# Attention decode on one core: K of a query in one load instead of two, and the output projection of all heads moved behind the last V

## The chip, the core and the metric

The kernel runs on one core of a Trainium2 chip. A core has a matrix engine (PE; loading its stationary operand is shown as PEld), a vector engine (DVE), a scalar engine (ACT), a general engine (POOL) and a sync engine (SP), which here does nothing but issue transfers. Transfers run on 16 DMA engines that all queues share. SBUF is the on-chip memory of 128 partitions, PSUM the 128-partition memory that PE writes. The metric is device microseconds (us) of one execution. 1 KB is 1024 bytes in the sizes of loads below; MB and GB/s are decimal.

## The reference, cut to what matters

One token for each of two batch rows goes through a pre-norm attention over a long cache and a bilinear gated feed-forward. All data are float32.

```python
B, D, H, Sk, Dh, F = 2, 448, 16, 8192, 256, 1792
q = (layernorm(x) @ wq).reshape(B, 1, H, Dh)            # one query a head and batch row
scores = einsum("bhqd,bhkd->bhqk", q, k_cache) * Dh**-0.5
o = einsum("bhqk,bhkd->bhqd", softmax(scores), v_cache)
h = x + o.reshape(B, 1, H * Dh) @ wo
n = layernorm(h)
out = h + ((n @ w_gate) * (n @ w_up)) @ w_down
```

K and V are 16 heads x 2 batch rows x 8192 x 256 float32 each, 268 MB each. Everything else is 24 MB.

## The kernel before, in words

The program is one stream of 32 queries (`NQ`), a query being one head `h` and one batch row `b`. SP issues every large load in program order, and a load waits in SP's queue until the buffer that it overwrites is free; all that is queued behind it on SP waits too.

**Buffers.** `ring` holds four buffers of 32 KB a partition. A query takes all four in turn: two halves of K (`load_k`, 4096 KB each) and two halves of V (`load_v`, 4096 KB each; the last V goes in four loads of 2048 KB). Query weights and output weights of two heads come together, 1792 KB every fourth query (`load_w`, two buffers of their own in `wpool`).

**One query.** PE computes the scores from a K half as it lands (`scores`, L185: 16 matmuls of 512 columns a half, four of them side by side on 32 columns of the array each; a float32 matmul shows as two records, so a half is "x32" in the profile). The 8192 scores lie as 128 partitions x 2048 in one PSUM tile `s` of four banks. DVE takes the maximum of each half (L241), PE transposes the two results (L245), DVE reduces and negates (L247), PE spreads it to all partitions (L251), ACT copies it (L253) and computes the exponentials `p` with their row sums (L255). Then DVE multiplies V with `p` and sums, eight instructions of 128x2048 a query (L263). Around every second query PE also computes the next head's query vectors (`queries`, L165 and L168).

**Output projection.** When both queries of a head are done, `output` finishes it between the two score halves of the next query: row sums (L195), reciprocal (L197), the sum over partition groups (L200), the division (L204), and ten matmuls that add the head's share into `acc_ps` (L210, stationary operand 128x128 weights, moving operand 2 columns). The last head's `output` stands behind the loop.

**Feed-forward.** `load_ff` puts the gate, up and down weights (3136 KB each) into `ring` buffers behind the last V. Then `hT` (L291), the second layer norm (`center`, `squares`, L295 to L300), gate projection (L312 on `wg_t`), its scale `rv` (L320 to L326), the residual into the result's PSUM (L333), up projection (L312 on `wu_t`), their product (L342), transposes (L344, L346), down projection (L351: 56 matmuls of 112 columns, the result on four column groups), copy (L358) and two output transfers (L361).

Of the kernel before, what the change touches and what calls it, by code (L numbers as in the profile page):

```python
# [14 lines left out]
EPS = 1e-5  # L15
P = 128
# [6 lines left out]
HK = GK // 2  # L23
NO = DH // R
MM = 512
RING = 4
WQ, WO = 3 * DH + P, 2 * D
WH = WQ + WO
# [5 lines left out]
OC = D // G  # L34
# [10 lines left out]
def tile_decode_block(  # L45
# [5 lines left out]
    wqo: bass.AP,  # L51
# [8 lines left out]

    nc = tc.nc
    const = ctx.enter_context(tc.tile_pool(name="const", bufs=1))
    ring = ctx.enter_context(tc.tile_pool(name="ring", bufs=RING))
    wpool = ctx.enter_context(tc.tile_pool(name="wpool", bufs=2))
# [6 lines left out]
    def load_w(hp):  # L71
        t = wpool.tile([P, 2, WH], F32, tag="w", name=f"w_{hp}")
        nc.sync.dma_start(t.rearrange("p h n -> p (h n)"), wqo[hp])
        return t

    def load_k(b, h):
        got = []
        for n in range(2):
            t = ring.tile([P, 2, G, HK], F32, tag="ring", name=f"k_{h}_{b}_{n}")
            nc.sync.dma_start(t.rearrange("p c g k -> p (c g k)"), kc[b, h, n])  # L80
            got.append(t)
        return got

    def load_v(b, h, parts):
        got = []
        for n in range(2):
            t = ring.tile([P, NO // 2, GK], F32, tag="ring", name=f"v_{h}_{b}_{n}")
            k = NO // 2 // parts
            for m in range(parts):
                nc.sync.dma_start(  # L90
                    t[:, m * k : (m + 1) * k, :].rearrange("p o k -> p (o k)"),
                    vc[b, h, n, :, m * k * GK : (m + 1) * k * GK],
                )
            got.append(t)
        return got
# [3 lines left out]
    w_now = load_w(0)  # L99
# [3 lines left out]
    avg = const.tile([P, P], F32, name="avg")  # L103
    nc.vector.memset(avg, 1.0 / D)
    ones = const.tile([P, P], F32, name="ones")
    nc.vector.memset(ones, 1.0 / R)
    row = const.tile([1, P], F32, name="row")
    nc.vector.memset(row, 1.0)
# [5 lines left out]

    acc_ps = ps_1.tile([P, DC, B], F32, name="acc_ps")
# [12 lines left out]
    def center(h, tag):  # L128
        mean = ps_m.tile([P, B], F32, tag="sm", name=f"mean_{tag}")
        nc.tensor.matmul(mean, avg, over_chunks(h, f"h_{tag}"), start=True, stop=True)  # L130
        xc = const.tile([P, DC, B], F32, name=f"xc_{tag}")
        nc.vector.tensor_sub(xc, h, mean[:, None, :].to_broadcast([P, DC, B]))
        return xc
# [8 lines left out]
    nc.tensor.matmul(var, avg, squares(xc, "x"), start=True, stop=True)  # L142
    std = const.tile([P, B], F32, name="std")
    nc.scalar.activation(std, var, AF.Sqrt, bias=eps_t, scale=1.0)
# [14 lines left out]
    def queries(h, w):  # L159
        wh = w[:, h % 2]  # L160
        ps = ps_m.tile([P, 2, B], F32, tag="sm", name=f"q_ps_{h}")
        for c in range(2):
            for k in range(DC - 1):
                at = k * DH + c * P
                nc.tensor.matmul(  # L165
                    ps[:, c, :], wh[:, at : at + P], xn[:, k, :], start=(k == 0), stop=False
                )
            nc.tensor.matmul(  # L168
                ps[:, c, :], wh[:, 3 * DH : WQ], xn[:, DC - 1 + c, :], start=False, stop=True
            )  # L170
        q = work.tile([P, 2, B, R], F32, tag="q", name=f"q_{h}")
# [8 lines left out]
    def scores(s, q, b, kt, n):  # L180
        for j in range(HK // MM):
            at = n * HK + j * MM
            for c in range(2):
                for g in range(G):
                    nc.tensor.matmul(  # L185
                        s[g * R : (g + 1) * R, at : at + MM],
                        q[:, c, b, :],
                        kt[n][:, c, g, j * MM : (j + 1) * MM],
                        start=(c == 0),
                        stop=(c == 1),  # L190
                    )

    def output(h, w, oacc, lsum):
# [9 lines left out]
        oT = work.tile([P, B, 2], F32, tag="oT", name=f"oT_{h}")  # L203
        nc.vector.tensor_mul(oT, oT_ps, rl[:, :, None].to_broadcast([P, B, 2]))  # L204
        for m in range(DC + 1):
            at = min(m, DC - 1)
            rows = slice(0, P) if m < DC - 1 else slice((m - at) * HALF, (m - at + 1) * HALF)
            for c in range(2):
                wo = w[:, h % 2, WQ + c * D : WQ + (c + 1) * D]
                nc.tensor.matmul(  # L210
                    acc_ps[rows, at, :], wo[:, at * P : at * P + rows.stop - rows.start],
                    oT[:, :, c], start=(h == 0 and m == 0 and c == 0),
                    stop=(h == H - 1 and c == 1),
                    skip_group_check=True,
                )
# [5 lines left out]
    for i in range(NQ):  # L221
        h, b = divmod(i, B)
        kt = load_k(b, h)
        if h % 2 == 1 and b == 0 and h + 1 < H:
            w_next = load_w((h + 1) // 2)
# [12 lines left out]
        mT = ps_m.tile([1, 2, P], F32, tag="sm", name=f"mT_{i}")  # L238
        m = work.tile([P, 2], F32, tag="m", name=f"m_{i}")
        for n in range(2):  # L240
            nc.vector.tensor_reduce(  # L241
                m[:, n : n + 1], s[:, n * HK : (n + 1) * HK], axis=AX.X, op=ALU.max
            )
        for n in range(2):
            nc.tensor.transpose(mT[:, n, :], m[:, n : n + 1], ident)  # L245
        nm = work.tile([1, 1], F32, tag="nm", name=f"nm_{i}")
        nc.vector.tensor_reduce(  # L247
            nm, mT.rearrange("o n p -> o (n p)"), axis=AX.X, op=ALU.max, negate=True
        )
        nb_ps = ps_m.tile([P, 1], F32, tag="sm", name=f"nb_ps_{i}")  # L250
        nc.tensor.matmul(nb_ps, row, nm, start=True, stop=True)  # L251
        nb = work.tile([P, 1], F32, tag="nb", name=f"nb_{i}")
        nc.scalar.activation(nb, nb_ps, AF.Copy)  # L253
        p = work.tile([P, GK], F32, tag="p", name=f"p_{i}")
        nc.scalar.activation(p, s, AF.Exp, bias=nb, scale=1.0, accum_out=lsum[:, b : b + 1])  # L255

        if b == B - 1 and h + 1 < H:
            w_of = w_next if h % 2 == 1 else w_now
            q_next = queries(h + 1, w_of)

        for o in range(NO):
            v = vt[o // (NO // 2)][:, o % (NO // 2), :]
# [3 lines left out]
        if b == B - 1:  # L266
            last = (h, w_now, oacc, lsum)
            if h + 1 < H:
                q_now = q_next
                w_now = w_of  # L270

    def load_ff(w, name, cuts):
        t = ring.tile([P, NF * D], F32, tag="ring", name=name)
        for a, z in zip((0,) + cuts, cuts + (NF * D,)):
            nc.sync.dma_start(t[:, a:z], w[:, a:z])
        return t

    wg_t = load_ff(wg, "wg_t", ())
    wu_t = load_ff(wu, "wu_t", (2 * F, 3 * F))
    wd_t = load_ff(wd, "wd_t", (8 * D, 11 * D, 13 * D))  # L280

    ff = ps_s.tile([P, 4, MM], F32, tag="s", name="ff_ps")
    g_ps, u_ps, y_ps = ff[:, 0], ff[:, 1], ff[:, 3, :OC]
    hm_ps = ff[:, 2].rearrange("p (n k) -> p n k", k=P)
    for t in (g_ps, u_ps):
        nc.vector.memset(t[2 * 32 :, FG[2] :], 0.0)
    nc.vector.memset(y_ps, 0.0)

    output(*last)
    hT = const.tile([P, DC, B], F32, name="hT")  # L290
    nc.vector.tensor_add(hT, xT, acc_ps)  # L291
# [7 lines left out]
    sr = const.tile([P, 4, B, 16], F32, name="sr")  # L299
# [18 lines left out]
    project(g_ps, wg_t)  # L318
    var = ps_m.tile([P, 1], F32, tag="sm", name="var_h")
    nc.tensor.matmul(var, sr.rearrange("p g b r -> p (g b r)"), avg[:, 0:1], start=True, stop=True)  # L320
    ve = const.tile([P, 1], F32, name="ve")
    nc.vector.tensor_scalar_add(ve, var, EPS)
    rv = const.tile([P, 1], F32, name="rv")
    nc.vector.reciprocal(rv, ve)
    g_sb = const.tile([P, MM], F32, name="g_sb")
    nc.scalar.activation(g_sb, g_ps, AF.Copy, scale=rv)  # L326

    for q in range(G):
        at = q * OC
        while at < (q + 1) * OC:  # L330
            c, k = divmod(at, P)
            n = min(P - k, (q + 1) * OC - at)
            nc.tensor.matmul(  # L333
                y_ps[32 * q : 32 * q + B, at - q * OC : at - q * OC + n],
                hT[:, c, :], ident[:, k : k + n], start=(at == q * OC), stop=False,
                skip_group_check=True,
            )
            at += n

    project(u_ps, wu_t)  # L340
    hm = const.tile([P, MM], F32, name="hm")
# [6 lines left out]
    for g in range(4):  # L348
        for n in range(FG[g] // P):
            for q in range(G):  # L350
                nc.tensor.matmul(  # L351
                    y_ps[32 * q : 32 * q + B, :], hmT[:, n, g, :],
                    wd_t[:, k * D + q * OC : k * D + (q + 1) * OC],
# [3 lines left out]
    y = const.tile([P, OC], F32, name="y")  # L357
    nc.vector.tensor_copy(y, y_ps)  # L358
    rows = y.rearrange("(q r) d -> r q d", r=32)
    for b, e in ((0, nc.sync), (1, nc.scalar)):  # L360
        e.dma_start(out[b, 0].rearrange("(q d) -> q d", q=G), rows[b])  # L361
# [5 lines left out]
def pack(np, inputs):  # L367

# [10 lines left out]
    k = np.asarray(inputs["A_k_cache"]).reshape(B, H, G, 2, HK, 2, P)  # L379
    got["kc"] = np.ascontiguousarray(k.transpose(0, 1, 3, 6, 5, 2, 4)).reshape(  # L380
        B, H, 2, P, 2 * G * HK
    )
    v = np.asarray(inputs["A_v_cache"]).reshape(B, H, G, GK, 2, NO // 2, R)
    got["vc"] = np.ascontiguousarray(v.transpose(0, 1, 4, 2, 6, 5, 3)).reshape(
        B, H, 2, P, NO // 2 * GK
    )
    wq, wo = np.asarray(inputs["A_wq"]), np.asarray(inputs["A_wo"])
# [46 lines left out]
```

## Time and profile before

| what | value |
|---|---|
| median of 3 runs | 1323.71 us (1323.62 to 1325.27) |
| the profiled execution, its own time | 1324.97 us |
| its span | 1323.2 us |
| mean granted TensorE clock | 0.636 of full |
| busy: PE, DVE, ACT | 38%, 51%, 6% of the span |
| HBM read | 561.19 MB, 424 GB/s over the span |
| loads on SP's queue | K 64, V 66, weights 16 |

"Busy" is the time in which an engine executes. In the view of 40 slices each digit is the busy share of one fortieth of the span in tenths. In the chain of work that ended last each row is start, duration and what; "x32" counts records. In a view of windows each row is the window, its length, busy time (records in brackets) of the engines named, the granted clock, the DMA engines' busy share and GB/s. The profiled execution is 1.3 us above the median of the runs.

### The profile page before, as it was taken

The page shows a single profiled execution, that of the slowest core. Times are in us where ns is not written, and L with a number is a line of the kernel's source. Part 1 is how long each engine was busy: PE and PEld are TensorE (multiplying, and loading weights), DVE is VectorE, ACT ScalarE, POOL GpSimd, SP SyncE. Part 2 cuts the span into 40 slices and gives each one's busy share as a digit, 9 for nine tenths or more (in the row PEclk, how much of TensorE's full clock was granted, in tenths as well). Part 3 has the DMA queues.
Part 4 walks back from the last instruction along what each step waited for, and adds up shares of the span by engine and source line. Part 5 has one row for each costly group of instructions (what it writes and reads, how often), then busy time and mean ns, then how long its engine had stood idle before and what let it go on. Part 6 is the DMA issues. An engine that isn't in the chain of part 4 may idle for free.

```text
span 1323.2 us, 7506 instructions
## 1 busy us (share of the span) xinstructions
PE 499.9 (38%) x3114; PEld 200.2 (15%) x3114; DVE 669.7 (51%) x674; ACT 79.3 (6%) x116; POOL 0.8 (0%) x8
## 2 busy tenths in 40 slices
PE   4133542425434134431335424244342244423235
PEld 2011210202112011110112102111020111101113
DVE  0664355653455654455644456643456633556643
ACT  0100000000000000000000000000000000000000
POOL 0000000000000000000000000000000000000000
PEclk9666665666666566675576655666565666656777
DMA  9999999999999999999999999999999999999995
GB/s 401 428 436 426 435 430 431 427 435 430 428 433 429 433 430 431 428 432 430 432 432 429 432 430 429 429 433 429 429 433 432 429 431 431 429 428 434 433 422 214
DMA packets 21217, 561.67 MB, mean 424 GB/s; under 512 B 2496, under 2 KB 2624, under 8 KB 3136
## 3 DMA queue, kind: packets, MB, share of 16 engines
q1 hardware_dynamic: 21032, 561.20, 98.8%
q8 instruction: 24, 0.39, 0.1%
q14 instruction: 9, 0.07, 0.0%
q10 hardware_dynamic: 152, 0.01, 0.0%
HBM read 561.19 MB, written 0.00 MB: 424 GB/s over the span
## 4 chain that ended last, share of the span: by engine, by line
DMA 83%; PE 15%; DVE 2%; issue 0%; ACT 0%; SPq 0%; DVEq 0%; ACTq 0%
DMA k<-in_kc_dram 83%; PE s L185 13%; DVE v L263 1%; PE ff_ps L312 1%; PE acc_ps L210 0%; PE ff_ps L351 0%; DVE m L241 0%; ACT p L255 0%; DVE hm L342 0%; ACT g_sb L326 0%; PE ff_ps L344 0%; PE mean_h L130 0%; DVE nm L247 0%; SPq L80 0%; PE ff_ps L333 0%
## 5 line engine op out<-in xcount | busy, mean ns | idle before, releaser
L263 DVE SCALAR_TENSOR_TENSOR v<-v,p 128x2048 f32<-128x2048 f32 x256 | 569.5, 2287 | 120.1 <-ACT p L255 70.6
L185 PE MATMUL s<-k,q 128*32 128x512 f32 x2048 | 360.7, 869 | 693.8 <-DMA k<-in_kc_dram 693.8
L241 DVE TENSOR_REDUCE m<-s 128x1 f32<-128x1024 f32 x64 | 75.4, 1219 | 403.8 <-PE s L185 403.8
L185 PEld LDWEIGHTS s<-k,q 128*32 128x32 f32 x2048 | 87.0, 152 | 925.9 <-issue 822.6
L253 ACT ACTIVATE nb<-nb_ps 128x1 f32<-128x1 f32 x32 | 5.5, 171 | 1174.1 <-PE nb_ps L251 1174.1
L255 ACT ACTIVATE p<-s,nb 128x2048 f32<-128x2048 f32 x32 | 62.9, 1967 | 1.2 <-ACT nb L253 0.2
L197 DVE RECIPROCAL rl<-l_ps 128x2 f32<-128x2 f32 x16 | 2.7, 169 | 83.4 <-PE l_ps L195 83.4
L245 PE MATMUL mT<-ident,m 128*1 128x128 f32 x64 | 18.2, 284 | 70.8 <-DVE m L241 70.8
L165 PE MATMUL q_ps<-xn,w 128*128 128x2 f32 x192 | 40.2, 325 | 0.8 <-PE var_x L142 0.8
L165 PEld LDWEIGHTS q_ps<-xn,w 128*128 128x128 f32 x192 | 38.2, 290 | 1.1 <-PE var_x L142 0.9
L210 PE MATMUL acc_ps<-oT,w 128*128 128x2 f32 (+1 forms) x320 | 31.1, 239 | 6.3 <-DVE oT L204 6.3
L210 PEld LDWEIGHTS acc_ps<-oT,w 128*128 128x128 f32 (+1 forms) x320 | 29.5, 179 | 7.9 <-DVE oT L204 7.7
L251 PE MATMUL nb_ps<-nm,row 1*128 1x1 f32 x64 | 15.9, 316 | 16.2 <-DVE nm L247 16.2
L245 PEld LDWEIGHTS mT<-ident,m 128*1 128x1 f32 x64 | 5.1, 79 | 109.0 <-DVE m L241 109.0
L263 DVE DVE_READ_ACCUMULATOR v<-v,p 128x1 f32 x256 | 20.9, 82 | 0.0
L247 DVE TENSOR_REDUCE nm<-mT 1x1 f32<-1x256 f32 x32 | 13.2, 412 | 12.5 <-PE mT L245 12.5
L251 PEld LDWEIGHTS nb_ps<-nm,row 1*128 1x128 f32 x64 | 13.2, 256 | 23.1 <-DVE nm L247 23.1
L168 PE MATMUL q_ps<-xn,w 128*128 128x2 f32 x64 | 16.7, 330 | 0.0
L168 PEld LDWEIGHTS q_ps<-xn,w 128*128 128x128 f32 x64 | 15.8, 302 | 0.0
L200 PE MATMUL oT_ps<-oacc,gsum 128*32 128x4 f32 x128 | 4.8, 184 | 16.4 <-DVE v L263 16.4
L195 PEld LDWEIGHTS l_ps<-lsum,ones 128*128 128x128 f32 x32 | 5.0, 195 | 15.0 <-issue 12.6
L195 PE MATMUL l_ps<-lsum,ones 128*128 128x2 f32 x32 | 6.3, 268 | 2.4 <-ACT p L255 2.4
(63 smaller groups left out, 52.0 us busy)
## 6 DMA issues: line engine op xcount, KB each, us to landing
k<-in_kc_dram SPq DMA_DIRECT2D x64, 4096.0 KB, 33.4
v<-in_vc_dram SPq DMA_DIRECT2D x62, 4096.0 KB, 29.8
w<-in_wqo_dram SPq DMA_DIRECT2D x8, 1792.0 KB, 37.5
v<-in_vc_dram SPq DMA_DIRECT2D x4, 2048.0 KB, 27.4
wg_t<-in_B_w_gate_dram SPq DMA_DIRECT2D x1, 3136.0 KB
wu_t<-in_B_w_up_dram SPq DMA_DIRECT2D x1, 1792.0 KB
wd_t<-in_wd_dram SPq DMA_DIRECT2D x1, 1792.0 KB, 18.8
wu_t<-in_B_w_up_dram SPq DMA_DIRECT2D x1, 896.0 KB, 27.9
```

The costliest lines, as they stand in the source:

```text
L165: nc.tensor.matmul(ps[:, c, :], wh[:, at : at + P], xn[:, k, :], start=(k == 0), stop=False)
L168: nc.tensor.matmul(ps[:, c, :], wh[:, 3 * DH : WQ], xn[:, DC - 1 + c, :], start=False, stop=True)
L185: nc.tensor.matmul(s[g * R : (g + 1) * R, at : at + MM], q[:, c, b, :], kt[n][:, c, g, j * MM : (j + 1) * MM], start=(c == 0), stop=(c == 1),)
L195: nc.tensor.matmul(l_ps, ones, lsum, start=True, stop=True)
L210: nc.tensor.matmul(acc_ps[rows, at, :], wo[:, at * P : at * P + rows.stop - rows.start], oT[:, :, c], start=(h == 0 and m == 0 and c == 0) ...
L241: nc.vector.tensor_reduce(m[:, n : n + 1], s[:, n * HK : (n + 1) * HK], axis=AX.X, op=ALU.max)
L245: nc.tensor.transpose(mT[:, n, :], m[:, n : n + 1], ident)
L247: nc.vector.tensor_reduce(nm, mT.rearrange("o n p -> o (n p)"), axis=AX.X, op=ALU.max, negate=True)
L251: nc.tensor.matmul(nb_ps, row, nm, start=True, stop=True)
L255: nc.scalar.activation(p, s, AF.Exp, bias=nb, scale=1.0, accum_out=lsum[:, b : b + 1])
L263: nc.vector.scalar_tensor_tensor(v, v, 1.0, p, op0=ALU.mult, op1=ALU.mult, accum_out=oacc[:, b, o : o + 1])
L312: nc.tensor.matmul(ps[32 * g : 32 * g + 32, : FG[g]], xs.rearrange("p b r -> p (b r)"), w[:, at : at + FG[g]], start=(c == 0), stop=(c == ...
```

## The change

K of a query becomes one tile of 64 KB a partition with one buffer (`kbuf`), loaded by one transfer of 8192 KB. V of a query becomes one tile of 64 KB a partition with two buffers (`vbuf`), loaded by one transfer of 8192 KB (the last V by two of 4096 KB). Each head's query weights come alone, 448 KB a head in one buffer. `output` shrinks to `head_out`, which stores the normalized head in `oT`, and runs behind all scores of the next query instead of between two halves. The output weights of all heads (7168 KB) are loaded behind the last V into K's buffer, in two halves of 3584 KB, and `project_out` multiplies them behind the loop, with `oT` as the stationary operand and 448 weight columns moving, on four column groups, followed by a copy and five matmuls that sum the groups and transpose (`hT_ps`). The maximum of a query becomes one instruction over 2048 scores. Gate and up weights share one V buffer, down weights take the other. The down projection is done in two column groups of 224 columns instead of four of 112, and one transfer writes the result. The constants `avg` and `row` are replaced by scaled uses of `ones`.

```diff
+    kbuf = ctx.enter_context(tc.tile_pool(name="kbuf", bufs=1))
+    vbuf = ctx.enter_context(tc.tile_pool(name="vbuf", bufs=2))
+    one = ctx.enter_context(tc.tile_pool(name="one", bufs=1))
...
+    def load_wq(h):
+        t = one.tile([P, WQ], F32, tag="wq", name=f"wq_{h}")
+        nc.sync.dma_start(t, wq[h])
...
     def load_k(b, h):
...
+        t = kbuf.tile([P, 2, G, GK], F32, tag="k", name=f"k_{h}_{b}")
+        nc.sync.dma_start(t.rearrange("p c g k -> p (c g k)"), kc[b, h])
+        return t
     def load_v(b, h, parts):
...
+        t = vbuf.tile([P, NO, GK], F32, tag="v", name=f"v_{h}_{b}")
...
+    oT = const.tile([P, H, 2, B], F32, name="oT")
+    acc_ps = ps_1.tile([P, D], F32, name="acc_ps")
+    nc.vector.memset(acc_ps, 0.0)
...
         kt = load_k(b, h)
-        if h % 2 == 1 and b == 0 and h + 1 < H:
-            w_next = load_w((h + 1) // 2)
+        if b == 0 and h + 1 < H:
+            w_now = load_wq(h + 1)
         vt = load_v(b, h, 2 if i == NQ - 1 else 1)
...
-        scores(s, q_now, b, kt, 0)
+        scores(s, q_now, b, kt)
         if last is not None:
-            output(*last)
+            head_out(*last)
             last = None
-        scores(s, q_now, b, kt, 1)
...
+    wo_t = kbuf.tile([P, H * WO], F32, tag="k", name="wo_t")
+    n = H * WO // 2
+    for m in range(2):
+        nc.sync.dma_start(wo_t[:, m * n : (m + 1) * n], wo[:, m * n : (m + 1) * n])
+    gu_t = vbuf.tile([P, 2, WF], F32, tag="v", name="gu_t")
+    wd_t = vbuf.tile([P, NF * D], F32, tag="v", name="wd_t")
...
+    def project_out(heads):
+        for h in heads:
+            for c in range(2):
+                j = 2 * (h % 2) + c
+                k = h * 2 + c
+                nc.tensor.matmul(
+                    acc_ps[32 * j : 32 * j + B, :], oT[:, h, c, :],
+                    wo_t[:, k * D : (k + 1) * D], start=(h < 2), stop=(h >= H - 2),
+                )
+
+    project_out(range(H - 1))
+    head_out(*last)
+    project_out((H - 1,))
+    nc.vector.tensor_copy(acc_sb, acc_ps)
...
+        nc.tensor.matmul(
+            hT_ps[rows, at, :], acc_sb[:, at * P : at * P + k], gsum[:, :B],
+            start=True, stop=True,
+        )
...
-            for q in range(G):
+            for ps, a in ((ya_ps, 0), (yb_ps, YC)):
                 nc.tensor.matmul(
-                    y_ps[32 * q : 32 * q + B, :], hmT[:, n, g, :],
-                    wd_t[:, k * D + q * OC : k * D + (q + 1) * OC],
+                    ps, hmT[:, n, g, :], wd_t[:, k * D + a : k * D + a + YC],
```

On SP's queue at the end of the program (each row a load, destination and source, partitions x elements a partition), before:

```order
L80 DMA k_1_0_2613<-in_kc_dram 128x8192
L80 DMA k_1_1_2615<-in_kc_dram 128x8192
L90 DMA v_1_0_2617<-in_vc_dram 128x4096 x2
L90 DMA v_1_1_2620<-in_vc_dram 128x4096 x2
L275 DMA wg_t<-in_B_w_gate_dram 128x6272
L275 DMA wu_t<-in_B_w_up_dram 128x3584
L275 DMA wu_t<-in_B_w_up_dram 128x1792
L275 DMA wu_t<-in_B_w_up_dram 128x896
L275 DMA wd_t<-in_wd_dram 128x3584
```

and after:

```order
L80 DMA k_1_2279<-in_kc_dram 128x16384
L87 DMA v_1_2281<-in_vc_dram 128x8192 x2
L244 DMA wo_t<-in_wo_dram 128x7168 x2
L251 DMA gu_t<-in_B_w_gate_dram 128x3584
L251 DMA gu_t<-in_B_w_gate_dram 128x2688
L251 DMA gu_t<-in_B_w_up_dram 128x3584
L251 DMA gu_t<-in_B_w_up_dram 128x1792
L251 DMA gu_t<-in_B_w_up_dram 128x896
L251 DMA wd_t<-in_wd_dram 128x3584
```

Two loads of output weights now stand between the last V and the feed-forward weights.

In the loop, SP's queue for the two queries of a head, before (a head at which a pair of heads' weights is loaded):

```order
L80 DMA k_0_0_2205<-in_kc_dram 128x8192
L80 DMA k_0_1_2207<-in_kc_dram 128x8192
L73 DMA w_2209<-in_wqo_dram 128x3584
L90 DMA v_0_0_2211<-in_vc_dram 128x8192
L90 DMA v_0_1_2213<-in_vc_dram 128x8192
L80 DMA k_1_0_2293<-in_kc_dram 128x8192
L80 DMA k_1_1_2295<-in_kc_dram 128x8192
L90 DMA v_1_0_2297<-in_vc_dram 128x8192
L90 DMA v_1_1_2299<-in_vc_dram 128x8192
```

and after, with the waits in brackets (a wait on PE is for K's or the query weights' last reader, on DVE for V's, on DMAHW for the earlier load into the same buffer):

```order
L80 DMA k_0_2071<-in_kc_dram 128x16384 [waits DMAHW6_49,PE_49]
L75 DMA wq_2073<-in_wq_dram 128x896 [waits DMAHW4_49,PE_49]
L87 DMA v_0_2075<-in_vc_dram 128x16384 [waits DMAHW5_49,DVE_49]
L80 DMA k_1_2142<-in_kc_dram 128x16384 [waits DMAHW0_49,PE_49]
L87 DMA v_1_2144<-in_vc_dram 128x16384 [waits DMAHW7_49,DVE_49]
```

Every load of K now waits until the scores of the query just before have read the whole of K; the load of the next head's query weights stands between K and V and waits for `queries` of the head before it.

On PE behind the last softmax, before:

```order
L195 MATMUL l_ps_2693<-lsum_2536,ones 128x2
L200 MATMUL oT_ps_2697<-oacc_2535,gsum 32x4 x4
L210 MATMUL acc_ps<-oT_2702,w_2209 128x2 x6
L210 MATMUL acc_ps<-oT_2702,w_2209 64x2 x4
L130 MATMUL mean_h<-sum_h_h,avg 128x2
L312 MATMUL ff_ps<-wg_t,xr 32x512 x2
```

and after:

```order
L269 MATMUL acc_ps<-wo_t,oT 2x448 x30
L186 MATMUL l_ps_2384<-lsum_2215,ones 128x2
L191 MATMUL oT_ps_2388<-oacc_2214,gsum 32x4 x4
L269 MATMUL acc_ps<-wo_t,oT 2x448 x2
L286 MATMUL hT_ps<-gsum,tail 128x2 x3
L286 MATMUL hT_ps<-gsum,tail 64x2 x2
L123 MATMUL total_h<-sum_h_h,ones 128x2
L319 MATMUL var_h<-ones,tail 128x1
```

The last head's finish now stands behind 30 matmuls on the output weights of the other heads, and the second norm's variance (L319) now stands ahead of the gate projection.

More of the change, by code (lines that the diff above doesn't have):

```diff
@@ L178, in queries, with scores @@
         return q
-    def scores(s, q, b, kt, n):
-        for j in range(HK // MM):
-            at = n * HK + j * MM
+    def scores(s, q, b, kt):
+        for j in range(GK // MM):
+            at = slice(j * MM, (j + 1) * MM)
             for c in range(2):
@@ L202, in output @@
             )
[L203 to L215, printed above, removed]
+        nc.vector.tensor_mul(
+            oT[:, h].rearrange("p c b -> p b c"), oT_ps, rl[:, :, None].to_broadcast([P, B, 2])
+        )
     q_now = queries(0, w_now)
@@ L266, in tile_decode_block @@
         if b == B - 1:
[L267 to L273, printed above, removed]
+            last = (h, oacc, lsum)
+    wo_t = kbuf.tile([P, H * WO], F32, tag="k", name="wo_t")
[3 more added lines that the diff above has]
+    gu_t = vbuf.tile([P, 2, WF], F32, tag="v", name="gu_t")
@@ new lines, in tile_decode_block @@
+    project_out(range(H - 1))
+    head_out(*last)
+    project_out((H - 1,))
+    tail = one.tile([P, GK], F32, tag="p", name="tail")
+    acc_sb, g_sb, hm = tail[:, :D], tail[:, MM : 2 * MM], tail[:, 2 * MM : 3 * MM]
+    y = tail[:B, 3 * MM : 3 * MM + D]
+    nc.vector.tensor_copy(acc_sb, acc_ps)
+    hT_ps = ps_m.tile([P, DC, B], F32, tag="sm", name="hT_ps")
+    for m in range(DC + 1):
+        at = min(m, DC - 1)
+        rows = slice(0, P) if m < DC - 1 else slice((m - at) * HALF, (m - at + 1) * HALF)
+        k = rows.stop - rows.start
+        nc.tensor.matmul(
+            hT_ps[rows, at, :], acc_sb[:, at * P : at * P + k], gsum[:, :B],
+            start=True, stop=True,
+        )
@@ L356, in tile_decode_block @@
             k += 1
[L357 to L361, printed above, removed]
+    nc.vector.tensor_copy(y[:, :YC], ya_ps)
+    nc.scalar.activation(y[:, YC:], yb_ps, AF.Copy)
+    nc.sync.dma_start(out.rearrange("b s d -> (b s) d"), y)
 _OUTS = [((B, 1, D), "float32")]
```

162 lines of the change are left out of this document (61 added, 101 removed).

## The prediction

> **What bounds the kernel now.** I read the slices first, then one window over the steady part, then the chain that ended last, then the end of the stream of loads. Part 2 of the page and a window from the first query's scores to the last's (PE, PEld, DVE, ACT and POOL busy, granted clock, DMA share, GB/s):
>
> ```profile
> DVE  0664355653455654455644456643456633556643
> DMA  9999999999999999999999999999999999999995
> 27.81:1268.10 1240.29, 463.64 (x2798) 180.64 (x2799) 642.85 (x619) 74.54 (x109) 0.00 (x0) 0.63 1.00 431
> ```
>
> The DMA engines are never idle for 1240 us, at 431 GB/s, while no other engine passes 52%. So up to the last K the time is bytes over rate, plus what each load costs beside its bytes. The chain shows the beat (start of the scores of a query's second half of K, and their duration):
>
> ```profile
> 27.81 5.38 PE s L185 x32
> ...
> 709.21 6.64 PE s L185 x32
> 748.11 5.38 PE s L185 x32
> 791.29 6.56 PE s L185 x32
> ...
> 1229.21 3.69 PE s L185 x32
> 1268.10 5.38 PE s L185 x32
> ```
>
> A query without a weight load takes 38.90 us (748.11 - 709.21) for four loads of 4096 KB, one with the 1792 KB load 43.18 us. So 4096 KB cost 9.725 us and 1792 KB 4.28 us: 0.00236 us a KB, and 0.05 us left over for each load. The stream's end gives a second value (issues of the down weights, first and last start, and time to landing; then PE busy, clock, DMA share and GB/s):
>
> ```profile
> L275 SPq DMA_DIRECT2D wd_t<-in_wd_dram x4: 327/431/433, 1288.4 to 1289.7; - x4
> DMA to landing us min/median/max: 18.8/20.4/20.8
> 1304.00:1305.00 1.00, 1.00 (x10) 0.50 0.72 296
> 1308.00:1309.00 1.00, 1.00 (x8) 0.50 0.49 190
> 1309.00:1310.00 1.00, 1.00 (x6) 0.95 0.23 88
> ```
>
> The last load lands at 1289.7 + 20.8 = 1310.5, which is 42.4 us after the last K for 17,600 KB in 12 loads: 41.5 us of bytes, 0.07 a load. I take 0.055. What the kernel pays behind the stream is the chain's end:
>
> ```profile
> 1273.51 2.36 DVE m L241 x2
> ...
> 1279.40 3.52 DVE v L263 x3
> ...
> 1283.83 13.37 DVE v L263 x13
> ...
> 1298.34 3.29 PE acc_ps L210 x20
> 1301.65 0.17 DVE hT L291
> ...
> 1303.35 6.47 PE ff_ps L312 x28
> ...
> 1311.76 3.47 PE ff_ps L312 x22
> 1315.32 0.70 DVE hm L342
> 1317.00 2.91 PE ff_ps L351 x112
> 1319.93 0.28 DVE y L358
> ```
>
> From the last K (1268.1) on nothing waits for a transfer any more: softmax to 1279.4, V on DVE to 1297.2, then 23 us of small serial work. The stream ended 12.7 us before the span does (1323.2). The change has to be judged by how it rearranges these two, and by whether it keeps the stream full.
>
> **The change part by part.**
>
> *Output weights behind the last V.* The bytes stay the same, but 7168 KB move from before the last K to behind the last V. Eight loads of 1792 KB (8 x 4.28 = 34.3 us) become sixteen of 448 KB (16 x 1.11 = 17.8): the last K lands 16.5 us earlier.
>
> *Fewer, larger loads.* Up to the last K there are 126 loads of K and V, then 63: 63 x 0.055 = 3.5 us earlier. Over the whole program 146 loads become 92, 54 x 0.055 = 3.0 us. No row has a 64 KB row of a partition, so this is bounded: nothing saved if the cost belongs to bytes of a row and not to the load, 5.4 us at 0.1 a load. The w loads with 14 KB rows and the K loads with 32 KB rows lie on one line, so I see no reason for a loss in the trace; that is a rival below. Last K: 1268.1 - 16.5 - 3.5 = 1248.1.
>
> *K with one buffer.* The next K can be issued only when all scores of this query are done. A half takes 3.69 to 6.64 us, a whole 7.4 to 13.3, say 10. At the program's start the engines go from the first issue to a full rate within about 3.3 us:
>
> ```profile
> 0.73 0.40 SPq L73 DMA_DIRECT2D w<-in_wqo_dram  x1
> 1.00:2.00 1.00, 0.00 (x0) 0.00 (x0) 0.27 (x3) 0.82 (x1) 0.42 (x3) 1.00 0.59 115
> 4.00:5.00 1.00, 0.00 (x0) 0.00 (x0) 0.00 (x0) 0.00 (x0) 0.00 (x0) 1.00 1.01 417
> ```
>
> So K is under way at the latest 16.6 us after the previous K landed, while this query's V keeps the engines busy for 2 x 9.7 = 19.4 us. The cover is V's transfer, with 2.8 us to spare at the slowest scores and 6 at the mean; what is behind K on SP (weights, V) has longer. Some engines end up to 5 us ahead of others (the windows from 1304 to 1310), so the foremost may run dry now and then; the hindmost set the landing and do not. Cost: nothing. [...]
>
> *V in one load.* DVE starts on V when all of it has landed, 19.4 us after K, no longer at 9.7 or after the softmax. Eight instructions take 17.8 us (1279.40 to 1297.19), so it ends 37.2 us after K, before the next V is due (58), and V has a second buffer. Cost: nothing, except for the last V, which still comes in halves.
>
> *Query weights with one buffer.* Their load waits for `queries`, which follows the softmax by a few us, inside the 19 us of K's own transfer. Nothing. One maximum and one transpose a query less: about 0.3 us off a part of the query that waits for V anyway. Nothing.
>
> *The end, from the last K at 1248.1.* Scores 10, softmax 5.9: V starts on DVE at 1264.0 and ends at 1281.8 (V's second half lands at 1267.5, in time). The output weights are issued at 1258, long before V has landed, and follow it without a gap: 8.51 us each, 1276.0 and 1284.6. Gate lands at 1292.1, up at 1299.6, down in four pieces to 1307.3. From the second half of the output weights PE and DVE are the path:
>
> ```profile
> 1226.13 1.84 PE L210 MATMUL acc_ps<-oT,w 128*128 128x2 f32 x20 [0.36 <-DVE oT L204]
> 1225.21 0.38 PE L195 MATMUL l_ps<-lsum,ones 128*128 128x2 f32 x2
> 1304.20 0.23 DVE L300 COPY sr<-sum_sq_h 128x128 f32<-128x128 f32 x1
> 1311.36 0.40 PE L333 MATMUL ff_ps<-ident,hT 128*2 128x112 f32 x14 [1.23 <-ACT g_sb L326]
> ```
>
> 1. Heads 8 to 14: 14 matmuls of 448 columns, four side by side, against 16 of 512 in 5.38 us (3.69 to 6.64): x 0.77 = 4.1 (2.8 to 5.1).
> 2. Row sums and last head: 0.9 us at 1225.21 to 1226.13, here 1.1; its two matmuls 0.8.
> 3. Copy of 128x448 out of PSUM: 0.70 for 512 columns (L342), here 0.65. Five matmuls where L210 had ten: 1.84 to 3.29 for ten, here 1.4 (0.9 to 1.65).
> 4. `hT` to the copied squares: 1301.65 to 1304.43, 2.8. Variance and residual, now ahead of the gate: 0.9. That is 11.8 so far: 1296.4, and gate has landed.
> 5. Gate projection 6.47 at the clock of 0.50, 3.47 at 1.00; between, 5.0. In the windows the clock rose 5.7 us after the projection began, so I take the second value for up: 3.5, to 1304.9; its weights are there.
> 6. Product to transposed: 1315.32 to 1317.00, 1.7.
> 7. Down projection: 112 columns took 2.91 on four column groups; twice the columns on two groups, 5.8 (by the number of instructions alone it would be half of 2.91). To 1312.4, behind the last load by 5 us.
> 8. Copy of half of the result on each of two engines 0.4, and 3.0 from its end to the span's (1320.21 to 1323.2).
>
> Sum: 1315.8, against 1323.2 of the same execution: 7.4 us less, 0.56%. The median of the runs stands 0.5 above that span, so 1316.3. Of what the last K gains (20 us), 12.6 are spent: the output weights' 17 us take the place of 16 us of V on DVE, and the new matmuls, the variance and the two-group down projection are longer than what they replace.
>
> **The rivals.**
>
> *A, no cheaper loads:* the 0.055 us belongs to a row's bytes, or a row of 64 KB is moved in two pieces. All else as above: +3.0, 1319.3. For it: the cost rests on two differences of a few hundredths. Against it: both point the same way.
>
> *B, the end at one clock.* If PE stays at 1.00 from the output weights on, items 1, 2, 3 and 5 lose 4 us: 1312.3. If it stays at 0.50 into the up projection, they gain 5.5: 1321.8. For the slow end: in the windows PE sat at 0.50 for 5.7 us of steady work. Against: there are 10 us of steady work here before the up projection ends.
>
> *C, K's single buffer opens a gap each query:* the slower case. It begins where scores and start of transfer take more than 19.4 us, and decides against the change at 7.4 / 31 = 0.24 us a query: 19.7 us against at most 16.6 that I find. At 1 us a query it gives 1347, with nothing covered (10 us a query) 1626. For it: SP's queue runs one load ahead where it ran three, as K's landing time shows:
>
> ```profile
> k<-in_kc_dram SPq DMA_DIRECT2D x64, 4096.0 KB, 33.4
> xT<-in_x_dram ACTq DMA_DIRECT2D x1, 4.0 KB, 7.8
> L120 DVE TENSOR_REDUCE sum_h_x<-xT x1: 160/160/160, 8.5 to 8.5; 128x2 f32<-128x6 f32 x1
> 14.74 0.57 PE L168 MATMUL q_ps<-xn,w 128*128 128x2 f32 x2
> ```
>
> (33.4 us for a transfer of 9.7.) Against it: the 19.4 us of V.
>
> *D, a gap at the start.* The 4 KB of `x` need 7.8 us beside the first weights, and the first query vectors end 6.8 us after `x` is there (8.5 to 15.3). Now the second weights and the first V stand in SP's queue behind those query vectors, and K's 64 KB rows follow a shorter weight load. If `x` waits for K's rows and lands after about 14 us (14 + 6.8 + up to 3.3 for a start, against the end of K's first load near 24), the stream stops once; at 18 us that is 4 us: 1320.3. Against it: `x` is issued as early as the weights. [...]
>
> *E, rows of 64 KB move more slowly:* 0.6% of 1300 us eats the gain. No row speaks for it.
>
> **How the numbers follow.** My forecast, 1316.3 with its own range 1313.5 to 1319, has 0.5; A 0.15; B 0.07 fast and 0.07 slow; C 0.05; D 0.12; E 0.04. The range holds all but C, E and the far ends of B and D: from the fast clock with 0.1 us a load (1312.3 - 2.4 = 1309.9) to the slow clock (1321.8): 1310 to 1322. No change means within 0.2% (2.6 us), about what a measurement tells here: 1321.1 to 1326.4. Forecast, A, fast B and most of D are faster (0.84); slow B, a part of D and of E are the same (0.09); C and the rest of E slower (0.07).
>
> **What would show it.** In the profile after: a DMA share of 1.00 and some 38.8 us from one query's scores to the next's; no long wait of PE on K beyond that; last K near 1248; V ending on DVE before the second half of the output weights lands; a down projection of 5 to 6 us; the last load landing near 1307, behind it 5 us of PE. The prediction fails if SP waits on PE for K while the DMA share drops in the slices (C), if the first V comes late (D), or if the beat per query is 39 us or more (A, E).

## The result and the profile after

The changed kernel takes 1316.52 us, the median of 4 runs (1315.25 to 1318.05), against 1323.72 for the kernel before on the same chip: a ratio of 0.9943 (95% interval 0.9926 to 0.9961), 7.2 us less. The profiled execution is the shortest of the four, 1315.25 us with a span of 1313.1; the other spans are 1314.2, 1314.4 and 1315.9.

The page of the changed kernel (span, the slices of DMA, the queue of the large loads, and the landing times of K and `x`):

```profile
span 1313.1 us, 6671 instructions
...
DMA  9999999999999999999999999999999999999996
...
q1 hardware_dynamic: 13252, 561.19, 99.1%
...
k<-in_kc_dram SPq DMA_DIRECT2D x32, 30.0
...
xT<-in_x_dram ACTq DMA_DIRECT2D x1, 4.0 KB, 3.2
```

The stream is as full as before, for 561.19 MB that now come in 13,252 packets (the page of before has 21,032). A row of 64 KB went as one packet: counted with one packet a row, the loads have 11,776 rows (8064 of them in the 63 loads of whole K and V), and 16 packets more for each of the 92 loads make 13,248. That a load has 16 packets more than its rows shows in e3 below: 63 loads more over the same rows, 1008 packets more (14,260). `x` landed 3.2 us after its issue, where it took 7.8.

The chain that ended last, in the loop (start and duration of a query's scores):

```profile
23.75 8.97 PE s L179 x64
...
63.59 9.53 PE s L179 x64
...
1168.32 8.43 PE s L179 x64
...
1207.04 9.50 PE s L179 x64
...
1245.76 8.96 PE s L179 x64
```

A query without a weight load takes 38.72 us (1245.76 - 1207.04; 38.90 before), one with the 448 KB load 39.84 (63.59 - 23.75; before, 43.18 with 1792 KB). From the first scores to the last 1222.01 us pass, where 1240.29 did. What SP's queue waited for (us in total, times, longest):

```profile
SPq L80 <- DMA k<-in_kc_dram: 808.5, 31, 30.8
SPq L80 <- PE l_ps L186: 146.0, 15, 10.5
SPq L80 <- PE s L179: 144.1, 16, 9.6
```

Every K is issued some 10 us after the one before it landed. A window from 400 to 1200 us shows that this opened no gap (PE, PEld, DVE, ACT and POOL busy, clock, DMA share, GB/s):

```profile
400.00:1200.00 800.00, 225.54 (x1600) 88.90 (x1600) 420.95 (x391) 47.05 (x70) 0.00 (x0) 0.61 1.00 433
```

The end in the timeline (start, duration, engine, line, operation; in brackets the idle time before and its releaser):

```profile
1278.13 0.08 DVE L235 DVE_READ_ACCUMULATOR v<-v,p 128x1 f32 x1
...
1282.14 3.17 PE L269 MATMUL acc_ps<-wo_t,oT 128*2 128x448 f32 x28 [3.77 <-DMA wo_t<-in_wo_dram]
...
1287.14 0.62 DVE L280 COPY tail<-acc_ps 128x448 f32<-128x448 f32 x1 [1.02 <-PE acc_ps L269]
1287.82 1.04 PE L286 MATMUL hT_ps<-gsum,tail 128*128 128x2 f32 x10 [0.73 <-DVE tail L280]
...
1291.66 0.56 PE L319 MATMUL var_h<-ones,tail 128*128 128x1 f32 x2 [1.70 <-DVE tail L300]
...
1299.54 3.63 PE L312 MATMUL ff_ps<-gu_t,xr 128*32 128x512 f32 x32 [0.87 <-ACT tail L336]
```

V is off DVE at 1278.2, 3.9 us before the second half of the output weights lands; from there on the new serial work runs. Its last part in the chain:

```profile
1293.07 5.66 PE ff_ps L312 x22
...
1298.80 0.70 ACT tail L336
...
1299.54 3.69 PE ff_ps L312 x24
...
1305.00 0.35 PE ff_ps L347
...
1310.46 0.06 PE acc_ps L347
1310.54 0.35 ACT tail L353
```

The load of the down weights (first and last issue; time to landing), and PE's clock before and in the gate projection (window, length, PE busy, clock, DMA share, GB/s):

```profile
L251 SPq DMA_DIRECT2D wd_t<-in_wd_dram x4: 327/328/431, 1278.2 to 1286.4; - x4
...
DMA to landing us min/median/max: 18.5/22.8/24.6
```

```profile
1287.00:1288.00 1.00, 0.27 (x4) 1.00 0.98 401
1288.00:1289.00 1.00, 0.86 (x10) 1.00 0.94 394
1289.00:1290.00 1.00, 0.35 (x2) 1.00 0.97 409
1290.00:1291.00 1.00, 0.00 (x0) 0.74 1.05 437
1291.00:1292.00 1.00, 0.34 (x2) 0.50 1.06 437
1292.00:1293.00 1.00, 1.00 (x16) 0.50 1.06 444
1297.00:1298.00 1.00, 1.00 (x10) 0.85 1.03 428
```

The last of these loads, the smallest, took 18.5 us and landed at 1304.9 (1286.4 + 18.5), 8.2 us before the span's end; 12.7 us lay there before.

### The profile page after: what moved, and what is told of

Its sections match the earlier page's. It is cut to its first block, busy times and chain, and to the rows that moved or that the text cites. A ratio compares the mean times of both kernels' runs of the same rounds, so it can differ in the third digit from the quotient of the medians.

```text
span 1313.1 us, 6671 instructions
## 1 busy us (share of the span) xinstructions
PE 392.9 (30%) x2776; PEld 154.9 (12%) x2776; DVE 662.2 (50%) x641; ACT 79.0 (6%) x117; POOL 0.8 (0%) x8
## 3 DMA queue, kind: packets, MB, share of 16 engines
q1 hardware_dynamic: 13252, 561.19, 99.1%
HBM read 561.19 MB, written 0.00 MB: 427 GB/s over the span
## 4 chain that ended last, share of the span: by engine, by line
DMA 75%; PE 24%; issue 0%; DVE 0%; ACT 0%; SPq 0%; ACTq 0%; DVEq 0%
DMA k<-in_kc_dram 73%; PE s L179 22%; DMA wo_t<-in_wo_dram 2%; PE ff_ps L312 1%; PE ff_ps L347 0%; PE acc_ps L269 0%; PE l_ps L186 0%; PE hT_ps L286 0%; DVE tail L338 0%; ACT tail L336 0%; PE ff_ps L340 0%; DVE tail L280 0%; PE var_h L319 0%; DVE xr L295 0%; PE acc_ps L329 0%
## 5 line engine op out<-in xcount | busy, mean ns | idle before, releaser
L179 PE MATMUL s<-k,q 128*32 128x512 f32 x2048 | 290.3, 730 | 795.5 <-DMA k<-in_kc_dram 795.5
L218 DVE TENSOR_REDUCE m<-s 128x1 f32<-128x2048 f32 x32 | 73.2, 2286 | 194.9 <-PE s L179 194.9
L159 PE MATMUL q_ps<-xn,wq 128*128 128x2 f32 x192 | 34.2, 294 | 0.8 <-PE var_x L137 0.8
L220 PE MATMUL mT<-ident,m 128*1 128x128 f32 x32 | 10.0, 312 | 79.4 <-DVE m L218 79.4
L159 PEld LDWEIGHTS q_ps<-xn,wq 128*128 128x128 f32 x192 | 32.1, 247 | 1.1 <-PE var_x L137 0.9
L224 PE MATMUL nb_ps<-nm,ones 1*128 1x1 f32 x64 | 14.7, 297 | 11.9 <-DVE nm L222 11.9
L222 DVE TENSOR_REDUCE nm<-mT 1x1 f32<-1x128 f32 x32 | 8.9, 278 | 12.9 <-PE mT L220 12.9
L162 PE MATMUL q_ps<-xn,wq 128*128 128x2 f32 x64 | 15.4, 310 | 0.0
L269 PE MATMUL acc_ps<-wo_t,oT 128*2 128x448 f32 x64 | 8.8, 647 | 19.7 <-DMA wo_t<-in_wo_dram 19.3
L224 PEld LDWEIGHTS nb_ps<-nm,ones 1*128 1x128 f32 x64 | 12.0, 233 | 19.3 <-DVE nm L222 19.3
L162 PEld LDWEIGHTS q_ps<-xn,wq 128*128 128x128 f32 x64 | 14.2, 273 | 0.0
L312 PE MATMUL ff_ps<-gu_t,xr 128*32 128x384 f32 (+1 forms) x64 | 9.6, 698 | 0.9 <-ACT tail L336 0.9
L186 PEld LDWEIGHTS l_ps<-lsum,ones 128*128 128x128 f32 x32 | 4.8, 188 | 13.3 <-issue 13.3
## 6 DMA issues: line engine op xcount, KB each, us to landing
wd_t<-in_wd_dram SPq DMA_DIRECT2D x1, 1792.0 KB, 23.3
```

What stands on the lines that cost most here:

```text
L159: nc.tensor.matmul(ps[:, c, :], w[:, at : at + P], xn[:, k, :], start=(k == 0), stop=False)
L162: nc.tensor.matmul(ps[:, c, :], w[:, 3 * DH :], xn[:, DC - 1 + c, :], start=False, stop=True)
L179: nc.tensor.matmul(s[g * R : (g + 1) * R, at], q[:, c, b, :], kt[:, c, g, at], start=(c == 0), stop=(c == 1),)
L186: nc.tensor.matmul(l_ps, ones, lsum, start=True, stop=True)
L218: nc.vector.tensor_reduce(m, s, axis=AX.X, op=ALU.max)
L220: nc.tensor.transpose(mT, m, ident)
```

## The experiments

All start from the changed kernel. Ratios are to the kernel before on the same chip.

**e2_halves: K and V again in two loads each, all else as changed.**

```diff
-        nc.sync.dma_start(t.rearrange("p c g k -> p (c g k)"), kc[b, h])
+        n = G * GK
+        for m in range(2):
+            nc.sync.dma_start(
+                t[:, m].rearrange("p g k -> p (g k)"), kc[b, h, :, m * n : (m + 1) * n]
+            )
...
+        parts = 2
```

> The changed kernel, with each K and V (but the last V) loaded by two transfers into the two halves of each partition's 64 KB: rows of 32 KB again, 63 loads more, all else the same. Theory (a load or a row has a cost of its own beside its bytes): the beat of a query in the changed kernel is 38.73 us with two loads against 38.89 with four, so 0.08 us a load, 63 x 0.08 = 5.0 us more than the changed kernel: 1321.5. Rival A (the cost belongs to the bytes, the larger loads saved nothing): 1316.5.

Measured: 1322.61 us (1320.70 to 1322.76), ratio 0.9984 (0.9976 to 0.9993). The last two queries in its chain:

```profile
1212.16 8.63 PE s L184 x56
...
1251.05 8.01 PE s L184 x56
```

All of the change but the longer loads, the output weights' move above all, brings the last K from 1268.1 to 1251.05, 17 us earlier, and 1.7 us of that are left in the end. The other 5 to 6 us of the gain are in the size of the loads, or in the length of their rows. K has its single buffer here and the loads have the size of before, and the beat is that of before, 38.89 against 38.90 us: the single buffer itself costs nothing that shows.

**e7_rows32: one load each, but of 256 rows of 32 KB (two to a partition) instead of 128 rows of 64 KB.** It tells loads from rows.

```diff
-        nc.sync.dma_start(t.rearrange("p c g k -> p (c g k)"), kc[b, h])
+        nc.sync.dma_start(
+            t.rearrange("p c g k -> p c (g k)"), kc[b, h].rearrange("m p n -> p m n")
+        )
```

(V alike; K and V are laid out in memory to match.)

> The changed kernel with the same number of loads (one of 8192 KB for K, one for V), but K and V laid out in memory as two blocks, so that each load moves 256 rows of 32 KB instead of 128 of 64 KB. Two halves of a row in two loads cost 6.1 us more than the changed kernel (1322.6 against 1316.5). If that is the row's own cost (each row's start): the same here, 1322 to 1323. If it is the load's own: 1316.5.

Measured: 1321.46 us (1320.12 to 1324.24), ratio 0.9981 (0.9972 to 0.9990). Its chain's last two queries, and the packets of its queue:

```profile
1211.77 9.69 PE s L185 x64
...
1250.64 9.07 PE s L185 x64
```

```profile
q1 hardware_dynamic: 21316, 561.19, 99.2%
```

As many loads as the changed kernel, as many rows as the one before, and the time of the many rows: 38.87 us a query against 38.72. Two loads a query (e7) or four (e2, whose last query took 38.89) make no difference that shows. A query has 256 rows more here, 16 on each of 16 engines if they are spread evenly (their packets take 99.2% of all 16), so a row costs 0.15 / 16 = 0.01 us on its engine; the last K comes 4.9 us later, 63 x 8 = 504 rows an engine, 0.0097 each. The same price fits the short rows of the query weights: with 0.0094 us a row, the two beats give 0.002354 us a KB (16,384 KB and 16 or 32 rows an engine), so 448 KB in 8 rows an engine, of 3.5 KB each, should take 1.13 us, and 1.12 were measured (39.84 - 38.72). So by this estimate the price is a row's own, at all three lengths.

**e3_partitions: two loads of 64 partitions each, rows of 64 KB.**

```diff
+        for m in range(2):
+            rows = slice(m * HALF, (m + 1) * HALF)
+            nc.sync.dma_start(t[rows].rearrange("p c g k -> p (c g k)"), kc[b, h, rows, :])
```

(V alike.)

> The changed kernel, with each K and V (but the last V) loaded by two transfers of 64 partitions each: rows of 64 KB as in the changed kernel, but 63 loads more. If the fixed cost is the load's own (its issue, its completion): 5.0 us more than the changed kernel, 1321.5, the same as with two halves of each row. If it is the row's (128 rows a K or V in both kernels): no difference, 1316.5.

Measured: 2659.53 us (2655.17 to 2661.39), ratio 2.008 (2.005 to 2.011). Both theories missed it by a factor of two. A window of it:

```profile
600.00:1400.00 800.00, 115.41 (x800) 43.78 (x800) 187.82 (x176) 23.25 (x35) 0.00 (x0) 0.55 1.00 208
```

The engines are busy all the time and move 208 GB/s, 0.48 of 433. Why the rate halves is shown by no row here.

**e10_two_queues: the same halves, one on SP's queue and one on ACT's.**

```diff
+        for m, e in ((0, nc.sync), (1, nc.scalar)):
+            rows = slice(m * HALF, (m + 1) * HALF)
+            e.dma_start(t[rows].rearrange("p c g k -> p (c g k)"), kc[b, h, rows, :])
```

> The changed kernel with K and V loaded in halves of 64 partitions, the lower half issued by SP, the upper by ACT. All from SP, one behind the other, the same halves ran at 207 GB/s (2659.5 us). If a load of 64 partitions reaches only half of the paths into SBUF, two such loads in flight on two queues together reach all: near 430 GB/s, 1320 to 1400 (ACT issues its half of K later, behind its exponentials). If each engine is slow with rows of such a load whatever else runs: 2600 to 2700.

Measured: 2586.21 us, one run (1323.13 before).

```profile
600.00:1400.00 800.00, 119.18 (x800) 47.08 (x800) 203.11 (x189) 23.46 (x35) 0.00 (x0) 0.55 1.00 216
```

216 GB/s, with 296.95 MB moved by SP's queue and 264.25 MB by ACT's: having halves in flight from two queues doesn't bring the rate back. That refutes the first account, and the time lies just under the range of the second (2600 to 2700). Which resource halves the rate stays open.

**e5_scores2 and e6_scores3: the scores computed twice, and three times**, to find where K's single buffer runs out of cover.

```diff
-        for j in range(GK // MM):
+        for j in [*range(GK // MM)] * 2:
```

(In e6 the factor is 3.)

> The changed kernel, with the scores of each query computed twice over (same result): K's buffer is free 9.0 + 7.3 = 16.3 us after K lands instead of 9.0. Theory (the next K is covered by V's 19.4 us of transfer, as long as it is issued 2 to 3.3 us before V ends): at the edge of the cover, 0 to 0.2 us a query, 1316.5 to 1323. Rival C (K's single buffer already shows, each us of scores adds to each query): 7.3 x 31 = 226 us more, 1543.

> The changed kernel with the scores of each query computed three times over. With twice, K was issued 16.3 us after it landed and the kernel took 24 us more, 0.77 us a query: the cover ends at some 15.5 us of scores. Theory (beyond that edge each us of scores is a us of each query): 8.7 + 2 x 7.3 = 23.3 us of scores, 7.8 us a query beyond the edge, x 31 = 242, 1558. Rival (the loss is a share of the scores from the first us on, 24 / (7.3 x 31) = 11% of them): 48 us more, 1365.

Measured: twice 1340.46 us (1338.12 to 1341.96), ratio 1.0127 (1.0111 to 1.0142); three times 1490.79, one run (1323.13 before). The chains, first of e5, then of e6:

```profile
24.02 16.93 PE s L179 x128
...
1266.43 15.26 PE s L179 x128
```

```profile
829.75 22.48 PE s L179 x192
...
852.30 21.71 DMA k<-in_kc_dram
...
874.15 22.52 PE s L179 x192
...
1413.46 22.51 PE s L179 x192
```

And a window of e5:

```profile
100.00:1200.00 1100.00, 512.35 (x3989) 184.73 (x3993) 558.71 (x520) 63.14 (x94) 0.00 (x0) 0.69 0.99 425
```

With the scores computed twice (15.3 to 16.9 us a query) the last K lands 20.7 us later than in the changed kernel, 0.67 us a query; computed three times (22.2 to 23.8 us) it lands 167.7 us later, 5.4 us a query. The rest of the 24 and the 174 us that the two kernels lose comes behind the last K, where the last query's scores are longer too. In e6 the next K is issued after V has all landed (the DMA share is 0.12 from 848 to 850 us and 0.00 from 850 to 852), and lands 21.7 us later: 19.4 of bytes and 2.3 of start. A query there is 22.5 us of scores and 21.9 to the next landing, 44.4, which is 5.7 over 38.72, so by this run the cover ends at 22.5 - 5.7 = 16.8 us of scores. That e5 loses a little just below this edge fits engines that run dry one by one (DMA share 0.99); it was not separated further. The changed kernel's scores of 8.4 to 10.0 us stay 7 us clear of the edge, and 5 us below the shortest scores of e5. Of e6 the loss was put too high by two fifths (242 us against 174): I had taken the edge at 15.5 us, from all of e5's 24 us, and the scores at 23.3.

**e1_no_wo: without the output weights' load and their 32 matmuls.**

```diff
-    wo_t = kbuf.tile([P, H * WO], F32, tag="k", name="wo_t")
-    n = H * WO // 2
-    for m in range(2):
-        nc.sync.dma_start(wo_t[:, m * n : (m + 1) * n], wo[:, m * n : (m + 1) * n])
...
-    project_out(range(H - 1))
     head_out(*last)
-    project_out((H - 1,))
```

> The changed kernel without the load of the output weights and without their 32 matmuls (this leaves the output projection out: the attention's share of the result is zero). Theory (V's last work on DVE ends at 1278.1, and everything behind it but the 32 matmuls takes 27.9 us; the 17 us of weights hide under that work): the span ends at 1306.1, 7.0 us less than the changed kernel, 1309.5. Rival (the end is bound by the stream of weights): 17 us less, 1299.5.

Measured: 1308.98 us (1308.24 to 1309.26), ratio 0.9885 (0.9872 to 0.9899). Its chain:

```profile
1260.71 17.79 DVE v L235 x16
...
1286.09 6.02 PE ff_ps L296 x22
```

Without them V on DVE is the path to 1278.5, and the gate starts at 1286.0 instead of 1293.0. So 7168 KB, 17 us of the stream, cost with their matmuls 7.5 us by the medians where they now stand (6.5 by the profiled spans, 1313.1 against 1306.6): the rest lies beside V on DVE.

**e4_down4: down projection and residual on four column groups of 112 again.**

```diff
-            for ps, a in ((ya_ps, 0), (yb_ps, YC)):
+            for q in range(G):
                 nc.tensor.matmul(
-                    ps, hmT[:, n, g, :], wd_t[:, k * D + a : k * D + a + YC],
+                    y_ps[32 * q : 32 * q + B, :], hmT[:, n, g, :],
+                    wd_t[:, k * D + q * OC : k * D + (q + 1) * OC],
```

> The changed kernel, with the down projection and the residual on four column groups of 112 columns and two output transfers as in the kernel before. Theory (the end of the program is a serial chain behind the output weights, and the two-group form made its down projection 5.5 us instead of 2.9): 2.6 us less, the span's end at 1310.5 of the profiled 1313.1, the median 1313.9. Rival (the last down weights land at 1304.9, so the chain waits for them): at most 0.5 us less than the changed kernel, 1316.0.

Measured: 1313.70 us (1313.17 to 1314.34), ratio 0.9921 (0.9908 to 0.9935).

```profile
1305.40 2.91 PE ff_ps L349 x112
```

2.91 us instead of 5.5: two column groups cost 2.6 us, all of it on the path. The medians differ by 2.8 us, but the intervals of the two ratios overlap (0.9926 to 0.9961 for the changed kernel), so the price rests on the row.

**e8_warm: five matmuls of 256 columns whose result nobody reads, while PE waits between the output projection and the gate.**

```diff
+    def keep_warm(n):
+        for _ in range(n):
+            nc.tensor.matmul(warm, ident, wo_t[:, :256], start=True, stop=True)
```

One stands behind the output projection, one behind `hT_ps`, three behind the mean.

> The changed kernel with five matmuls of 256 columns into an unused PSUM bank, put where PE waits for DVE between the output projection and the variance (their result is not used). Theory (the gate projection of 5.7 us ran at the clock of 0.50 because PE did little between 1287 and 1292): the clock stays at 1.00, the gate projection takes 3.5 us, 2.2 us less, 1314.3. Rival (the five matmuls are themselves on the path, or the clock falls all the same): 1316.5 to 1318.

Measured: 1314.15 us (1312.44 to 1315.93), ratio 0.9925 (0.9912 to 0.9937). The output projection behind its second half of weights and the gate projection, then the clock in the one and before the other (columns as above):

```profile
1282.08 4.87 PE L269 MATMUL acc_ps<-wo_t,oT 128*2 128x448 f32 x28 [4.00 <-DMA wo_t<-in_wo_dram]
...
1293.95 3.62 PE L321 MATMUL ff_ps<-gu_t,xr 128*32 128x512 f32 x30
```

```profile
1284.00:1285.00 1.00, 1.00 (x12) 0.50 1.00 419
1292.00:1293.00 1.00, 0.99 (x5) 1.00 1.05 441
```

The gate takes 3.6 us instead of 5.8, at a granted clock of 1.00 (every window from 1290 to 1298). But in this execution the clock had fallen earlier, by 1284 (0.50 from 1284 to 1285), so the 28 matmul records of the output projection took 4.87 us instead of 3.17, and the span is only 1.1 us shorter (1312.0 against 1313.1). The runs reach from 1312.44 to 1315.93, and the ratio's interval overlaps with that of the changed kernel. So a gate at the full clock is worth 2.2 us of its own length, but that the five matmuls shorten the program is not shown: e9 below has two of them, and its gate takes 5.33 us.

The clock fell in the changed kernel between 1290 and 1291, after 3 us in which PE had 1.5 us of work and no idle stretch of 1 us. What makes it fall there is not shown.

**e9_best: what the experiments point to.** Four column groups, the output weights in three loads (8, 6 and 2 heads), the gate projection ahead of the variance, the up projection in a PSUM tile of its own, two idle matmuls.

```diff
+    for a, z in ((0, 8), (8, 14), (14, 16)):
+        nc.sync.dma_start(wo_t[:, a * WO : z * WO], wo[:, a * WO : z * WO])
...
+    u_ps = ps_1.tile([P, MM], F32, name="u_ps")
...
+    project(g_ps, wg_t)
```

> The changed kernel with a shorter end: down projection on four column groups; output weights in three loads of 8, 6 and 2 heads, so that less is left to multiply behind the last; gate projection ahead of the variance, the up projection into a PSUM bank of its own so that it does not wait for the gate's scaling, the residual behind it; two idle matmuls while PE waits. Theory: the serial end falls by 2.6 + 2 + 3 us or more and is then bounded by the last load (landed at 1304.9 in the changed kernel) with 0.5 us of PE, 0.3 of copy and 2.6 of output behind it: 4.8 us less, 1311.7; it cannot be lower, since the bytes are the same. Rival (the end is still serial): not below the four-group kernel's 1313.7.

Measured: 1310.55 us (1310.37 to 1310.92), ratio 0.9898 (0.9885 to 0.9912), 6 us below the changed kernel. Its chain now ends on the stream, and its gate is shown in front of it:

```profile
1289.58 5.33 PE L321 MATMUL ff_ps<-gu_t,xr 128*32 128x512 f32 x32
```

```profile
1282.29 22.25 DMA wd_t<-in_wd_dram
...
1304.59 0.57 PE ff_ps L357 x16
...
1305.61 0.27 DVE tail L363
```

Behind the last load, which lands at 1304.5, stand 1 us of matmuls, the copy and the output, 4 us in all. PE already waits for the down weights before it (1.57 and 0.35 us idle), so a shorter chain would gain no more, the slow gate included: the stream itself would have to end sooner.

## Why the prediction was right

1316.3 was predicted and 1316.52 measured. The agreement is closer than its terms.

- **Last K.** Predicted at 1248.1, landed at 1245.8. The output weights' 16.5 us hold: e2, without the longer loads, has it at 1251.05, 17.0 earlier. The second term, 3.5 us for 63 fewer loads, was 5.3 (1251.05 to 1245.76), and it belongs to rows, not to loads (e7): this step had the cost at the wrong place. In the trace of before every load had 128 rows, so a price a load and a price a row gave the same line there, and I chose the wrong owner. Rival A, nothing saved, is refuted (it was priced at 3.0 us by the loads of the whole program; the path runs through the last K, where the term is 3.5), and so is E: 433 GB/s against 431.
- **K's single buffer.** Costs nothing, as predicted, by the cover named. The margin was put at 2.8 to 6 us and is 7: scores take 8.4 to 10.0, not 7.4 to 13.3, and the start takes 2.3, not 3.3. Rival C begins at scores of 15 to 17 us (e5, e6). Nothing shows of the 10 us a query that rival C has with nothing covered: e2 keeps the beat of before (38.89 us against 38.90), and only e6, where the cover is gone, loses 5.4 us a query.
- **Start.** Rival D is refuted: `x` landed in 3.2 us, and the first K 4.1 us earlier than its second half did before (27.81 to 23.75), 3.2 of them (4.28 - 1.11) for the smaller weights ahead of it.
- **V and query weights.** Nothing, as predicted: V is off DVE 37.1 us after K landed (1207.04 to 1244.14; 37.2 predicted), and 32.4 us in the last query, whose V comes in halves.
- **The end.** From the second half of the output weights to the span's end 31.2 us were predicted (1284.6 to 1315.8) and 31.0 measured (1282.1 to 1313.1), but by terms that cancel. Items 1 to 4 were 0.9 us too long: the matmuls took 3.17 us instead of 4.1 (PE at a clock of 1.00 from 1282 to 1287) and the five that transpose 1.0 instead of 1.4, while variance and residual took 1.4 (1291.66 to 1293.07) instead of 0.9. The gate took 5.8 instead of 5.0, as PE's clock had just fallen (0.50 from 1291 on). A step was left out: the up projection waits for ACT's scaling of the gate (L336), 0.9 us of idle PE, which e9's own PSUM tile takes away. Down 5.5 against 5.8, the output 2.2 against 3.0.
- **Rival B** came out between its ends, in two parts: full clock in the output projection (1.00 from 1282 to 1287), half in the gate (0.50 from 1291 to 1297, 0.85 to 1298), full in the up projection (1.00 from 1299 to 1304). Where the clock falls differs between the profiled executions (in e8 it fell in the output projection), so this part of the sum is luck too.
- **The sum's offset.** The profiled span was predicted at 1315.8 and is 1313.1, 2.7 us less (last K 2.3, the rest 0.4). I set the median 0.5 us above the span, since the profiled execution of before was 1.3 above its median. That of after is 1.3 below its own, and a run's time is some 2.2 above its own span (1.8 for the profiled one of before). The two errors cancel; the forecast of the median was right partly by luck.
- **Where the expected gain went.** Of 22.3 us at the last K, 12.2 are given back: last K to span's end was 55.1 us and is 67.3. 12.6 were predicted. e1 and e4 name 9 to 10 of it: 6.5 to 7.5 for the output weights, 2.6 for the two column groups. The rest was not separated.

## What to carry to other kernels

Where DMA engines are never idle, a buffer less cost nothing here as long as other loads covered the time until the next one could be issued (38.89 us a query in e2 against 38.90 before; 5.4 us a query lost in e6, where the cover had ended); work out that cover in us before splitting or doubling a tile. With loads of some MB as here, make rows long rather than loads large (38.72 us a query in rows of 64 KB, 38.87 in rows of 32 KB with as many loads); keep all 128 partitions in each load (433 GB/s against 208 with 64), and judge work moved behind the stream by the path at the end: it is free only as far as something else is longer there (the output weights' 17 us of stream cost 7.5 us with their matmuls). Small serial steps behind the last load then decide: there halving the column groups cost 2.6 us, and a gate projection at a clock of 0.50 took 5.8 us instead of 3.6.

## What the hardware showed that was not expected

- A load of 64 partitions runs at half the rate (208 GB/s against 433) with all DMA engines shown busy (share 1.00), from one queue or two (216 GB/s).
- A row, one packet, costs by estimate about 0.01 us of its engine beside its bytes, at 3.5, 32 and 64 KB alike (0.0094 and 0.0097 us from e7); the number of loads costs nothing that shows here (38.89 us a query with four, 38.87 with two).
- A full DMA share doesn't mean a full rate: e3 has 1.00 at 208 GB/s, the changed kernel 1.00 at 433.
